# Attention and a two-layer MLP on one core: one PSUM tile with a free list, and key scores in three groups instead of four

## The chip, the cores and the metric

The kernel runs on one core of one Trainium2 chip. The metric is the device time of a run in microseconds (us); the time shown for a kernel is the median of its runs. TensorE is called PE here, VectorE DVE, ScalarE ACT, GpSimd POOL, and SyncE's DMA queue SP.

## The reference

Attention over 8 batches and 12 heads of 448 positions with head size 64, where queries and keys are RMS-normalised, and then two matrix products with a leaky ReLU between them:

```python
q_n, k_n = rmsnorm(q, g_q), rmsnorm(k, g_k)          # 8 x 12 x 448 x 64, over the last axis
scores = 1 / sqrt(64) * q_n @ k_n.T
attn = softmax(scores)
x = (attn @ v), heads joined                          # 3584 x 768
h = x @ w_in                                          # 768 x 2048
out = maximum(0.01 * h, h) @ w_out                    # 2048 x 768, float32
```

## The kernel before

**Units.** The work is cut into 24 units (NU), each of four heads of one batch; three units (NQ) make a batch. For a unit `load` brings 128 x 896 elements of q and of k, DVE and ACT normalise them (`prep_sq`, `prep_ssq`, `prep_rinv`, `prep_norm`, two and more units ahead), a transposing DMA (`prep_trd`) makes `qkT`, and `prep_g` scales the queries. Scores are made transposed, one key tile t of seven (NS) at a time: `score` (L199) issues four 64*64 matmuls for a tile, one for each head, into two banks of PSUM. I call these four a set. `ex` (L218) turns each set into `et` with one exp on ACT, 128 x 896 elements, biased by `eb`, a shift that `shift_max` and `shift_mm` derive from the first set.

**Stages.** A unit has four stages d = 0 to 3. In each, `qk` scores the key tiles `STEPS[d]`, that is 1, 2, 2 and 2 sets, which I call a group; `ex` follows. Then `fill` takes the next `PLAN[u - 3][d]` items (2 or 3 in most stages) from `queue`, the products of the batch before. An item is a block of matmuls on PE: `moe1` (L389) is six 128x448 matmuls into one bank `hps` and a `prelu` on ACT (L383) that empties it; `moe2` (L435) and `seven` (L485) are blocks of eight 128x384 matmuls, emptied by DVE adds and copies and one ACT copy (L518). After each item one small piece of work from the list `jobs` is issued (loads, normalising, `prep_g`, squares). Stage 0 also finishes the unit before: `pv_slot` (attn times v, 28 matmuls, L367, into the two banks of `pslot`), `zcol` (sums of et, into one bank `zc`), `shift_mm`, `pv_out` (L322, ACT copies pslot to SBUF) and `zcol_ln` (L327, ACT reads zc).

**Order.** All instructions are issued in the order of this program (`tc.manual_schedule`), so each engine's queue is written out by hand; semaphores alone decide when each goes.

**PSUM.** There are eight banks of 512 float32 per partition. Before, they are two pools: `slot` hands out pairs of banks under the tag sT with two buffers (four banks), in turn, for score sets, pslot and one sum; `aux` hands out single banks, four buffers in turn, for everything else. From the last batches on `hold` takes the four banks into a list, and `drop` gives them back.

Of the kernel before, what the change touches and what calls it, by code (L numbers as in the profile page):

```python
# [18 lines left out]
def kernel(  # L19
# [34 lines left out]

    held = []

    def aux(shape, dtype, name):
        if held:
            return held[0].pop(0)
        return psum.tile(shape, dtype, tag="aux", bufs=4, name=name)  # L60

    def hold():
        if not held:
            banks = [psum.tile([P, 512], FP32, tag="aux", bufs=4, name=f"bank{i}") for i in range(4)]
            held.append(banks)

    def drop(bank):
        if held:
            held[0].append(bank)

# [96 lines left out]
    def prep_norm(u, c=ALL, tis=BOTH):  # L167
        n = c[1] - c[0]
        for ti in tis:
# [3 lines left out]
                buf(u, "rinv")[:, ti, :, c[0]:c[1], None].broadcast_to([P, 2, n, D]), op=ALU.mult)  # L173

    def prep_tr(u, ti, copies):
        tp = aux([P, NS, P], FP16, "tp")
        for (lo, hi), copy in copies:
            for x in range(lo, hi):
                nc.tensor.transpose(tp[:, x, :], buf(u, "n16")[:, ti, x].rearrange("p a d -> p (a d)"), ident16)
            copy(buf(u, "qkT")[:, ti, lo:hi], tp[:, lo:hi], ti == 0)  # L180

    def prep_trd(u):
# [7 lines left out]
    def kT(u, r, a, t):  # L190
        return buf(u, "qkT")[64 * a:64 * a + 64, 1, t, 64 * r:64 * r + 64]

    def slot():
        return psum.tile([P, 2, 512], FP32, tag="sT", bufs=2, name="sT")

# [12 lines left out]

    def ex(u):
        s = st[u]  # L210
        if "et" not in s:
            s["et"] = epool.tile([P, NS, 2, S], FP16, tag="et", name="et")
        for t, sT in s["sT"]:
            if isinstance(sT, list):
                for a in range(2):
                    nc.scalar.activation(s["et"][:, t, a], sT[a][:, 0:S], AF.Exp, bias=s["eb"], scale=1.0)
            else:
                nc.scalar.activation(s["et"][:, t], sT[:, :, 0:S], AF.Exp, bias=s["eb"], scale=1.0)  # L218

    def score0(u):  # L220
        banks = [aux([P, 512], FP32, "s0") for a in range(2)]
        score(u, 0, banks)
        st[u]["sT"] = [(0, banks)]
# [16 lines left out]
    def shift_bank(u):  # L240
        st[u]["pb"] = aux([P, 512], FP32, "pb")

    def shift_mm(u):
        s = st[u]
        if u > 0 and "pslot" in st[u - 1]:
            pb = st[u - 1]["pslot"][:, :, S:S + 64]
            for x in range(2):
                nc.tensor.matmul(pb[:, x], onesp, s["dg"][:, 64 * x:64 * x + 64], start=True, stop=True)
            nc.vector.tensor_reduce(s["spare"][:, 510:511], pb, axis=AXL.XY, op=ALU.max)  # L249
        else:  # L250
            if "pb" not in s:
                shift_bank(u)
            pb = s["pb"]
            nc.tensor.matmul(pb[:, 0:P], onesp, s["dg"], start=True, stop=True)
            nc.vector.tensor_reduce(s["spare"][:, 510:511], pb[:, 0:P], axis=AXL.X, op=ALU.max)
        s["eb"] = small.tile([P, 1], FP32, tag="eb", name="eb")
        nc.vector.tensor_scalar(s["eb"], s["spare"][:, 510:511], -1.0, DELTA, op0=ALU.mult, op1=ALU.add)
# [41 lines left out]
    def zcol(u):  # L299
        s = st[u]  # L300
        s["zc"] = aux([P, 512], FP32, "zc")
        ets = z_tiles(u)
        for i, e in enumerate(ets):
            for y in range(2):
                for a in range(2):
                    c = 32 * (2 * y + a)
                    nc.tensor.matmul(s["zc"][c:c + 32, 0:HS], onesr, e[:, a, HS * y:HS * y + HS],  # L307
                                     start=(i == 0), stop=(i == len(ets) - 1))
# [7 lines left out]
    def pv_out(u):  # L316
        s = st[u]
        s["x32"] = zpool.tile([P, 2, S], FP32, tag="x32", name="x32")
        if u in (3, 4, 5, 6):
            nc.vector.tensor_copy(s["x32"], s["pslot"][:, :, 0:S])  # L320
        else:
            nc.scalar.copy(s["x32"], s["pslot"][:, :, 0:S])  # L322

    def zcol_ln(u):
# [24 lines left out]
    def zinv(u):  # L349
        s = st[u]  # L350
        s["rz"] = zpool.tile([P, 2, S], FP32, tag="rz", name="rz")
        if "zslot" in s:
            nc.scalar.activation(s["rz"], s["zslot"][:, :, 0:S], AF.Ln)
            nc.scalar.activation(s["rz"], s["rz"], AF.Exp, bias=0.0, scale=-1.0)
        else:
            for r in range(2):
                nc.scalar.activation(s["rz"][:, r], s["zt"][r][:, 0:S], AF.Ln)
                nc.scalar.activation(s["rz"][:, r], s["rz"][:, r], AF.Exp, bias=0.0, scale=-1.0)

    def pv(u, t0=0, t1=NS):  # L360
        s = st[u]
        if t0 == 0 and "pslot" not in s:
            s["pv"] = [aux([P, 512], FP32, "pv") for r in range(2)]
        for t in range(t0, t1):
# [20 lines left out]
    def moe1(b, ft):  # L385
        xt = xts[b]
        hps = aux([P, 512], FP32, "hps")
        for kt in range(KT):
            nc.tensor.matmul(hps[:, 0:S], win16[:, kt // 2, kt % 2, ts(ft, P)], xt[:, kt // 2, kt % 2],  # L389
                             start=(kt == 0), stop=(kt == KT - 1))  # L390
        prelu(b, gt[:, ft, 64 * (b % 2):64 * (b % 2) + S], hps[:, 0:S])
        drop(hps)
# [32 lines left out]
    def moe2(pair, t, half, part, late=False, cut=8):  # L425
# [3 lines left out]
        if part == 0:  # L429
            ost[1] = aux([P, 512], FP32, "op2")  # L430
        op2 = ost[1]
# [48 lines left out]
    def seven(pair, tt, nxt=None, last=False, mixed=False):  # L480
# [6 lines left out]
        def bank(name):  # L487
            g[name] = aux([P, 512], FP32, name)
            return g[name]
# [115 lines left out]
    def late1(b, tail, after):  # L605
# [32 lines left out]
        def get(n, s):  # L638
            g[n, s] = aux([P, 512], FP32, "hp")
            return g[n, s]  # L640

        def start():
            hold()
            if tail:
                for i in range(2):
                    drop(slot()[:, 0])
            for name in ("u", "v"):
# [52 lines left out]
    def push(b):  # L700
# [32 lines left out]
        else:  # L733
# [13 lines left out]
            "3232", "2222", "3323", "3232", "2322", "4356", "5232")  # L747
    STEPS = ((0,), (1, 2), (3, 4), (5, 6))

    def narrow(u):  # L750
# [35 lines left out]
    with tc.manual_schedule():  # L786
# [5 lines left out]
        load(2)  # L792
        gps = aux([P, 512], FP32, "gps")
        wbank = aux([P, 512], FP32, "warm")
        warm(32, wbank)
# [9 lines left out]
        prep_rinv(0, (0,))  # L805
        nc.vector.tensor_copy(gcol, gps[:, 0:1])
        prep_ssq(0, ALL, (1,))
        prep_rinv(0, (1,))
# [5 lines left out]
        def tr(u, ti, chunks, tp=None):  # L814
            if tp is None:
                tp = aux([P, NS, P], FP16, "tp")
            for c, copy in chunks:
                for x in range(*c):
                    nc.tensor.transpose(tp[:, x, :], buf(u, "n16")[:, ti, x].rearrange("p a d -> p (a d)"), ident16)
                copy(buf(u, "qkT")[:, ti, c[0]:c[1]], tp[:, c[0]:c[1]], ti == 0)  # L820
            return tp

        tr(0, 0, ((CA, acopy),))
        tr(0, 0, ((CB, acopy),))
        tpk = tr(0, 1, ((K0, vcopy),))
        warm(6, wbank)
        prep_sq(1, ALL, (0,))
        qk(0, STEPS[0])
        shift_max(0)
        tr(0, 1, ((K1, acopy),), tpk)  # L830
        prep_sq(1, ALL, (1,))
# [8 lines left out]
        warm(10, st[0]["pb"])  # L840
        shift_mm(0)
        prep_ssq(1)

# [19 lines left out]
        load_w_in(1024, 1024)  # L863
        wb = aux([P, 512], FP32, "warm")
        warm(12, wb)
        qk(0, (2,))
        ex(0)
        warm(8, wb)
        qk(0, (3,))
        ex(0)  # L870
        tr(1, 0, ((ALL, vcopy),))
        tpk = tr(1, 1, ((K0, vcopy),))
# [6 lines left out]
        shift_max(1)  # L879
        vcopy(*k1[0])  # L880
        shift_bank(1)
        qk(0, (5,))
# [24 lines left out]
        qk(1, (2,))  # L907
        warm(6, st[1]["pb"])
        ex(1)
        trn(2, 0, vcopy)  # L910
# [36 lines left out]
        trn(3, 0, vcopy)  # L947
        warm(8, st[2]["pb"])
        trn(3, 1, vcopy)
        xmul(1)  # L950
        prep_ssq(4, ALL, (1,))
        qk(2, (4,))
        ex(2)
        st[2]["zt"] = [aux([P, 512], FP32, "zt") for r in range(2)]
        zsum(2, 0, 3)
# [22 lines left out]
        for ft in range(2):  # L978
            prelu(0, gt[:, ft, 0:S], first[:, ft, 0:S])
        del queue[0:2]  # L980

        for u in range(3, NU):
            for d in range(4):
                if d > 0 or u > 3:
                    qk(u, STEPS[d])
                    if d == 0:
# [9 lines left out]
                        else:  # L996
# [3 lines left out]
                            zinv(u - 1)  # L1000
                    ex(u)
                    if d == 0 and narrow(u - 1):
# [67 lines left out]
                if d == 3 and 6 <= u < NU - 3:  # L1070
                    for ti in range(2):
                        job(prep_sq, u + 3, ALL, (ti,))
                fill(u, d, jobs)
        zsum_slot(NU - 1)
# [38 lines left out]
```

## Time and profile before

| what | value |
| --- | --- |
| runs of the kernel | 417.27, 414.97, 413.72 us; median 414.97 |
| span of the profiled execution | 410.6 us, first to last instruction |
| median of the runs less that span | 4.4 us |
| PE busy | 398.2 us (97%), 3840 matmuls |
| DVE busy | 307.2 us (75%) |
| ACT busy | 298.4 us (73%) |
| POOL busy | 69.1 us (17%) |
| granted TensorE clock, mean | 1.000 |
| exp of a score set (L218) | 166 times, mean 1010 ns |
| score matmuls in PSUM pairs (L199) | 664, mean 363 ns, four at a time |

The profiled execution has no time of its own beside its span; what lies around the span is the 4.4 us between it and the median, which belongs to other executions. Busy times overlap. Durations on ACT and DVE overlap the next instruction's by some 0.1 us, so exps that follow each other start 0.90 us apart. The end of a matmul is modelled; its start is recorded, so distances on PE are taken from start to start. Units 7 to 21 lie between 93 and 330 us of the span; one takes 14.7 to 16.9 us.

### The profile page before, as it was taken

Reading aid. Unit: us, or ns where it says so; the run is one execution under the profiler, and the core shown is the slowest. Engines: PE = TensorE matmul, PEld = TensorE weight load, DVE = VectorE, ACT = ScalarE, POOL = GpSimd, SP = SyncE. Lnnn points to the kernel's source line nnn. Section 1 sums busy time; section 2 is a strip of 40 time slices with the busy share of each in tenths; the row PEclk is TensorE's granted clock in tenths of the full one; section 3 lists DMA queues with packets and bytes.
Section 4 is the critical chain, followed back from the end, with each engine's and each line's share of the span. In section 5 each row is a group of like instructions: output and inputs, shape, how many; then the busy total and the mean of one; then the engine's idle time right before and its main releaser. Section 6 shows DMA issues by size and latency. Waiting matters only on the chain.

```text
span 410.6 us, 9395 instructions
## 1 busy us (share of the span) xinstructions
PE 398.2 (97%) x3840; PEld 219.7 (54%) x3840; DVE 307.2 (75%) x490; ACT 298.4 (73%) x470; POOL 69.1 (17%) x70
## 2 busy tenths in 40 slices
PE   8689999999999999999999999999999999999996
PEld 7455444454445544555445544455445557558963
DVE  5997789999788766767669667678568788658772
ACT  5998977677887699777986779967986657653600
POOL 1886433100020200020020200003001202000000
PEclk9999999999999999999999999999999999999999
DMA  5999999999565885577666896667662460032014
GB/s 192 264 255 253 232 234 236 232 190 200 136 156 95 232 224 106 149 196 169 155 151 77 216 201 143 164 127 170 196 114 46 121 152 17 7 80 77 2 44 111
DMA packets 72526, 62.87 MB, mean 153 GB/s; under 512 B 36388, under 2 KB 67620, under 8 KB 72484
## 3 DMA queue, kind: packets, MB, share of 16 engines
q1 hardware_dynamic: 61888, 50.08, 47.6%
q0 software_dynamic: 10272, 11.80, 18.4%
q8 instruction: 30, 0.49, 0.5%
q10 hardware_dynamic: 324, 0.39, 0.3%
q14 instruction: 12, 0.10, 0.1%
HBM read 45.61 MB, written 11.01 MB: 138 GB/s over the span
## 4 chain that ended last, share of the span: by engine, by line
PE 90%; DVE 4%; ACT 3%; DMA 1%; issue 1%; SPq 0%; DVEq 0%
PE hps L389 28%; PE sT L199 10%; PE sT L367 6%; PE op L435 6%; PE mc L485 5%; PE ma L485 5%; PE bank L485 5%; PE md L485 5%; PE bank L617 5%; PE zc L307 3%; PE mb L485 3%; ACT et L218 2%; PE sT L485 2%; PE bank L435 1%; DVE n L171 1%; DMA rk<-in_k_dram 1%
## 5 line engine op out<-in xcount | busy, mean ns | idle before, releaser
L218 ACT ACTIVATE et<-sT,eb 128x896 f16<-128x896 f32 x166 | 159.6, 1010 | 25.8 <-PE sT L199 13.5
L389 PE MATMUL hps<-xt,win 128*128 128x448 f16 x600 | 120.8, 353 | 0.0
L389 PEld LDWEIGHTS <-win 128*128 128x128 f16 x612 | 56.7, 98 | 57.9 <-issue 9.9
L383 ACT ACTIVATE gt<-hps 128x448 f16<-128x448 f32 x100 | 53.9, 558 | 3.8 <-PE hps L389 3.2
L199 PE MATMUL sT<-qkT 64*64 64x448 f16 x664 | 52.3, 363 | 4.0 <-ACT et L218 3.2
L159 DVE TENSOR_REDUCE ssq<-sq 128x14 f32<-128x896 f32 (+2 forms) x49 | 50.2, 1057 | 0.8 <-ACT sq L148 0.8
L485 PEld LDWEIGHTS <-sa 128*128 128x128 f16 x352 | 32.8, 98 | 26.0 <-issue 5.8
L128 POOL DMA_DIRECT2D vt<-in_v_dram x24 | 17.9, 746 | 166.4 <-PE sT L367 166.0
L322 ACT COPY x<-sT 128x896 f32<-128x896 f32 x16 | 14.5, 907 | 29.8 <-DVE sT L249 27.5
L199 PEld LDWEIGHTS <-qkT 64*64 64x64 f16 x672 | 15.4, 104 | 37.2 <-issue 32.5
L485 PEld LDWEIGHTS <-gt 128*128 128x128 f16 x264 | 25.3, 98 | 18.4 <-issue 2.1
L347 POOL TENSOR_TENSOR xt<-x,rz 128x896 f16<-128x896 f32 x9 | 19.5, 2170 | 80.8 <-DMA rz<-zs 73.5
L236 DVE TENSOR_REDUCE sT<-sT 128x1 f32<-128x896 f32 x22 | 24.1, 1096 | 11.4 <-PE sT L199 11.3
L367 PE MATMUL sT<-et,vt 64*64 64x448 f16 x560 | 29.9, 349 | 0.0
L171 DVE TENSOR_TENSOR n<-rq,rinv 128x896 f16<-128x896 f32 (+2 forms) x25 | 26.3, 1055 | 3.2 <-ACT rinv L165 3.2
L435 PE MATMUL op<-wout,gt 128*128 128x384 f16 x160 | 28.4, 327 | 0.0
L171 DVE TENSOR_TENSOR n<-rk,rinv 128x896 f16<-128x896 f32 (+2 forms) x26 | 27.5, 1065 | 0.0
L292 DVE TENSOR_TENSOR ea<-ea,et 128x896 f16<-128x896 f16 x25 | 15.6, 625 | 15.2 <-ACT et L218 14.3
L367 PEld LDWEIGHTS <-vt 64*64 64x64 f16 x672 | 20.3, 107 | 10.6 <-issue 0.4
L435 PEld LDWEIGHTS <-gt 128*128 128x128 f16 x192 | 17.7, 98 | 13.8 <-issue 3.2
L485 PE MATMUL ma<-wout,gt 128*128 128x384 f16 x128 | 23.5, 326 | 0.0
L292 DVE TENSOR_TENSOR ea<-et 128x896 f16<-128x896 f16 x14 | 9.4, 672 | 11.9 <-ACT et L218 11.9
(144 smaller groups left out, 548.4 us busy)
## 6 DMA issues: line engine op xcount, KB each, us to landing
rq<-in_q_dram SPq DMA_DIRECT2D x24, 448.0 KB, 3.9
rk<-in_k_dram SPq DMA_DIRECT2D x24, 448.0 KB, 4.9
out_dram<-ost SPq DMA_DIRECT2D x52, 192.0 KB, 3.5
rz<-zs SPq DMA_DIRECT2D x80, 112.0 KB, 2.3
vt<-in_v_dram POOLq DMA_DIRECT2D x24, 224.0 KB, 5.2
win<-in_moe_w_in_dram POOLq DMA_DIRECT2D x8, 384.0 KB, 14.3
wout<-in_moe_w_out_dram POOLq DMA_DIRECT2D x2, 1536.0 KB, 28.9
out_dram<-ost SPq DMA_DIRECT2D x4, 96.0 KB, 2.1
```

The source lines that it names most:

```text
L159: nc.vector.tensor_reduce(buf(u, "ssq")[:, ti, :, c[0]:c[1]], buf(u, f"sq{ti}")[:, :, c[0]:c[1]], axis=AXL.X, op=ALU.add)
L171: nc.vector.tensor_tensor(buf(u, "n16")[:, ti, c[0]:c[1]].rearrange("p s a d -> p a s d"), src[:, :, c[0]:c[1]], buf(u, "rinv")[:, ti, :, ...
L199: nc.tensor.matmul(banks[a][64 * r:64 * r + 64, 0:S].rearrange("p (t x) -> p t x", t=NS), kT(u, r, a, t), qT(u, r, a), start=True, stop=True)
L218: nc.scalar.activation(s["et"][:, t], sT[:, :, 0:S], AF.Exp, bias=s["eb"], scale=1.0)
L236: nc.vector.tensor_reduce(s["spare"][:, 511:512], sT[:, :, 0:S], axis=AXL.XY, op=ALU.max)
L292: nc.vector.tensor_tensor(s["ea"], s["et"][:, 0] if t == 1 else s["ea"], s["et"][:, t], op=ALU.add)
L367: nc.tensor.matmul(s["pv"][r][64 * a:64 * a + 64, 0:S], vts[u % NV][64 * r:64 * r + 64, a, t], s["et"][64 * r:64 * r + 64, t, a], start=(t ...
L383: nc.scalar.activation(dst, src, AF.Prelu, bias=0.0, scale=1.0, alpha=0.01)
L389: nc.tensor.matmul(hps[:, 0:S], win16[:, kt // 2, kt % 2, ts(ft, P)], xt[:, kt // 2, kt % 2], start=(kt == 0), stop=(kt == KT - 1))
L435: nc.tensor.matmul(op2[:, 0:HC], gt[:, ft, ds(col(t), P)], wout16[:, ft, ds(HC * half, HC)], start=(i == 0), stop=(i == FT - 1))
L485: nc.tensor.matmul(bank[:, 0:HC], a[:, f], b[:, f], start=(first and f == 0), stop=(f == HF - 1), skip_group_check=not first)
L617: nc.tensor.matmul(bank[:, HX * i:HX * i + HX].rearrange("p (t x) -> p t x", t=NS), w, x[:, kt], start=start, stop=(kt == HK - 1), skip_gr ...
```

## The change

All eight banks become one tile `banks`, with views `single` (a bank) and `double` (an aligned pair), and a list `free` of banks in the order in which they were given back. `aux` takes a bank, `slot` takes a pair of free neighbours, `drop` returns either; each place that reads a bank for the last time now drops it. Until unit 7 banks 0 to 3 are for `aux` and 4 to 7 for `slot`, as two separate halves; from unit 7 on (`shared`) both take from all eight. `slot` takes the pair whose later-freed bank was freed longest ago; `aux` prefers a bank whose neighbour is in use.

In units 7 to 21 (`tripled`) the sets are grouped by `TRIPLES`: key tile 0 in stage 0, tiles 1 to 3 in stage 1, none in stage 2, tiles 4 to 6 in stage 3. After a group of three the first two exps are issued at once, as before; the third is joined to the first entry of `jobs`, so that it comes after the first item of the stage. Which items and other jobs a stage has does not change.

```diff
-    held = []
-    def aux(shape, dtype, name):
-        if held:
-            return held[0].pop(0)
-        return psum.tile(shape, dtype, tag="aux", bufs=4, name=name)
...
+    banks = psum.tile([P, 8, 512], FP32, tag="banks", name="banks")
+    single = [banks[:, i] for i in range(8)]
+    double = [banks[:, 2 * i:2 * i + 2] for i in range(4)]
+    free = [3, 0, 2, 1, 4, 5, 6, 7]
+    shared = []
+
+    def mine(i):
+        return shared or i < 4
+
+    def aux():
+        can = [i for i in free if mine(i)]
+        if shared:
+            can = [i for i in can[:-1] if i ^ 1 not in free] or can
+        free.remove(can[0])
+        return single[can[0]]
+
+    def slot():
+        if shared:
+            can = [i for i in free if i ^ 1 in free]
+            last = {i // 2: n for n, i in enumerate(free) if i in can}
+        else:
+            last = {i // 2: n for n, i in enumerate(free) if i >= 4 and i ^ 1 in free}
+        x = min(last, key=lambda i: last[i])
+        for i in (2 * x, 2 * x + 1):
+            free.remove(i)
+        return double[x]
...
-    def ex(u):
+    def ex(u, most=NS):
...
-        for t, sT in s["sT"]:
+        for t, sT in s["sT"][:most]:
...
                 nc.scalar.activation(s["et"][:, t], sT[:, :, 0:S], AF.Exp, bias=s["eb"], scale=1.0)
+                drop(sT)
+        s["sT"] = s["sT"][most:]
...
             nc.scalar.copy(s["x32"], s["pslot"][:, :, 0:S])
+        drop(s["pslot"])
...
         def start():
-            hold()
             if tail:
-                for i in range(2):
-                    drop(slot()[:, 0])
+                shared.append(b)
...
     STEPS = ((0,), (1, 2), (3, 4), (5, 6))
+    TRIPLES = ((0,), (1, 2, 3), (), (4, 5, 6))
+
+    def tripled(u):
+        return 7 <= u < NU - 2
...
         for u in range(3, NU):
             for d in range(4):
+                if u == 7 and d == 0:
+                    shared.append(u)
                 if d > 0 or u > 3:
-                    qk(u, STEPS[d])
+                    qk(u, (TRIPLES if tripled(u) else STEPS)[d])
...
-                    ex(u)
+                    ex(u, 2)
...
+                if st[u]["sT"]:
+                    jobs[0:1] = [also(lambda: ex(u), *jobs[0:1])]
                 fill(u, d, jobs)
```

More of the change, by code (lines that the diff above doesn't have):

```diff
@@ L53, with drop @@
     psum = ctx.enter_context(tc.tile_pool(name="psum", bufs=1, space=bass.MemoryType.PSUM))
-    held = []
-    def aux(shape, dtype, name):
-        if held:
-            return held[0].pop(0)
-        return psum.tile(shape, dtype, tag="aux", bufs=4, name=name)
[L62 to L69, printed above, removed]
+    banks = psum.tile([P, 8, 512], FP32, tag="banks", name="banks")
[21 more added lines that the diff above has]
+        return double[x]
+    def drop(tile_):
+        for i in range(8):
+            if tile_ is single[i]:
+                assert i not in free
+                free.append(i)
+                return
+        x = [i for i in range(4) if tile_ is double[i]][0]
+        assert 2 * x not in free and 2 * x + 1 not in free
+        free.extend((2 * x, 2 * x + 1))
     ident16 = cst.tile([P, P], FP16)
@@ L173, in prep_norm, with as_tp @@
                 buf(u, "rinv")[:, ti, :, c[0]:c[1], None].broadcast_to([P, 2, n, D]), op=ALU.mult)
+    def as_tp(bank):
+        return bank.bitcast(FP16)[:, 0:NS * P].rearrange("p (t x) -> p t x", t=NS)
     def prep_tr(u, ti, copies):
-        tp = aux([P, NS, P], FP16, "tp")
+        bank = aux()
+        tp = as_tp(bank)
         for (lo, hi), copy in copies:
@@ L180, in prep_tr @@
             copy(buf(u, "qkT")[:, ti, lo:hi], tp[:, lo:hi], ti == 0)
+        drop(bank)
     def prep_trd(u):
@@ L191, in kT @@
         return buf(u, "qkT")[64 * a:64 * a + 64, 1, t, 64 * r:64 * r + 64]
-    def slot():
-        return psum.tile([P, 2, 512], FP32, tag="sT", bufs=2, name="sT")
     def score(u, t, banks):
@@ L216, in ex @@
                     nc.scalar.activation(s["et"][:, t, a], sT[a][:, 0:S], AF.Exp, bias=s["eb"], scale=1.0)
+                    drop(sT[a])
             else:
                 nc.scalar.activation(s["et"][:, t], sT[:, :, 0:S], AF.Exp, bias=s["eb"], scale=1.0)
+                drop(sT)
+        s["sT"] = s["sT"][most:]
     def score0(u):
-        banks = [aux([P, 512], FP32, "s0") for a in range(2)]
+        banks = [aux() for a in range(2)]
         score(u, 0, banks)
@@ L240, in shift_bank @@
     def shift_bank(u):
-        st[u]["pb"] = aux([P, 512], FP32, "pb")
+        st[u]["pb"] = aux()
     def shift_mm(u):
@@ L255, in shift_mm @@
             nc.vector.tensor_reduce(s["spare"][:, 510:511], pb[:, 0:P], axis=AXL.X, op=ALU.max)
+            if u >= 3:
+                drop(pb)
         s["eb"] = small.tile([P, 1], FP32, tag="eb", name="eb")
@@ L300, in zcol @@
         s = st[u]
-        s["zc"] = aux([P, 512], FP32, "zc")
+        s["zc"] = aux()
         ets = z_tiles(u)
@@ L353, in zinv @@
             nc.scalar.activation(s["rz"], s["zslot"][:, :, 0:S], AF.Ln)
+            drop(s["zslot"])
             nc.scalar.activation(s["rz"], s["rz"], AF.Exp, bias=0.0, scale=-1.0)
@@ L357, in zinv @@
                 nc.scalar.activation(s["rz"][:, r], s["zt"][r][:, 0:S], AF.Ln)
+                drop(s["zt"][r])
                 nc.scalar.activation(s["rz"][:, r], s["rz"][:, r], AF.Exp, bias=0.0, scale=-1.0)
@@ L362, in pv @@
         if t0 == 0 and "pslot" not in s:
-            s["pv"] = [aux([P, 512], FP32, "pv") for r in range(2)]
+            s["pv"] = [aux() for r in range(2)]
         for t in range(t0, t1):
@@ L386, in moe1 @@
         xt = xts[b]
-        hps = aux([P, 512], FP32, "hps")
+        hps = aux()
         for kt in range(KT):
@@ L429, in moe2 @@
         if part == 0:
-            ost[1] = aux([P, 512], FP32, "op2")
+            ost[1] = aux()
         op2 = ost[1]
@@ L487, in bank @@
         def bank(name):
-            g[name] = aux([P, 512], FP32, name)
+            g[name] = aux()
             return g[name]
@@ L638, in get @@
         def get(n, s):
-            g[n, s] = aux([P, 512], FP32, "hp")
+            g[n, s] = aux()
             return g[n, s]
         def start():
-            hold()
             if tail:
-                for i in range(2):
-                    drop(slot()[:, 0])
+                shared.append(b)
             for name in ("u", "v"):
@@ L792 @@
         load(2)
-        gps = aux([P, 512], FP32, "gps")
-        wbank = aux([P, 512], FP32, "warm")
+        gps = aux()
+        wbank = aux()
         warm(32, wbank)
@@ L806 @@
         nc.vector.tensor_copy(gcol, gps[:, 0:1])
+        drop(gps)
         prep_ssq(0, ALL, (1,))
@@ L815, in tr @@
             if tp is None:
-                tp = aux([P, NS, P], FP16, "tp")
+                tp = aux()
             for c, copy in chunks:
                 for x in range(*c):
-                    nc.tensor.transpose(tp[:, x, :], buf(u, "n16")[:, ti, x].rearrange("p a d -> p (a d)"), ident16)
-                copy(buf(u, "qkT")[:, ti, c[0]:c[1]], tp[:, c[0]:c[1]], ti == 0)
-            return tp
-        tr(0, 0, ((CA, acopy),))
-        tr(0, 0, ((CB, acopy),))
+                    nc.tensor.transpose(as_tp(tp)[:, x, :], buf(u, "n16")[:, ti, x].rearrange("p a d -> p (a d)"), ident16)
+                copy(buf(u, "qkT")[:, ti, c[0]:c[1]], as_tp(tp)[:, c[0]:c[1]], ti == 0)
+            return tp
+        drop(tr(0, 0, ((CA, acopy),)))
+        drop(tr(0, 0, ((CB, acopy),)))
         tpk = tr(0, 1, ((K0, vcopy),))
         warm(6, wbank)
+        drop(wbank)
         prep_sq(1, ALL, (0,))
@@ L829 @@
         shift_max(0)
-        tr(0, 1, ((K1, acopy),), tpk)
+        drop(tr(0, 1, ((K1, acopy),), tpk))
         prep_sq(1, ALL, (1,))
@@ L841 @@
         shift_mm(0)
+        drop(st[0]["pb"])
         prep_ssq(1)
@@ L863 @@
         load_w_in(1024, 1024)
-        wb = aux([P, 512], FP32, "warm")
+        wb = aux()
         warm(12, wb)
@@ L868 @@
         warm(8, wb)
+        drop(wb)
         qk(0, (3,))
         ex(0)
-        tr(1, 0, ((ALL, vcopy),))
+        drop(tr(1, 0, ((ALL, vcopy),)))
         tpk = tr(1, 1, ((K0, vcopy),))
@@ L880 @@
         vcopy(*k1[0])
+        drop(tpk)
         shift_bank(1)
@@ L908 @@
         warm(6, st[1]["pb"])
+        drop(st[1]["pb"])
         ex(1)
@@ L948 @@
         warm(8, st[2]["pb"])
+        drop(st[2]["pb"])
         trn(3, 1, vcopy)
@@ L953 @@
         ex(2)
-        st[2]["zt"] = [aux([P, 512], FP32, "zt") for r in range(2)]
+        st[2]["zt"] = [aux() for r in range(2)]
         zsum(2, 0, 3)
@@ L979 @@
             prelu(0, gt[:, ft, 0:S], first[:, ft, 0:S])
+        drop(first)
         del queue[0:2]
```

## The prediction

> **What bounds the kernel now.** I read the head of the page first, for the share of each engine, then the line of granted clock, then the chain that ended last.
>
> ```profile
> PE 398.2 (97%) x3840; PEld 219.7 (54%) x3840; DVE 307.2 (75%) x490; ACT 298.4 (73%) x470; POOL 69.1 (17%) x70
> ...
> PEclk9999999999999999999999999999999999999999
> ...
> PE 90%; DVE 4%; ACT 3%; DMA 1%; issue 1%; SPq 0%; DVEq 0%
> ```
>
> TensorE (PE) is busy for 97% of the span at a full granted clock, and 90% of the chain is PE; the DVE and ACT shares of it lie in the first 45 us. In the stretch that the change touches (units 7 to 21, 93 to 330 us) the view of waits of PE lists nothing at all. So time can come only from what PE itself spends, and can be lost only by making PE wait. Next the timeline of PE, unit 10:
>
> ```profile
> 143.58 0.23 PE L248 MATMUL sT<-dg,onesp 128*128 128x64 f16 x2
> 143.65 2.44 PE L389 MATMUL hps<-xt,win 128*128 128x448 f16 x12
> 146.01 0.57 PE L199 MATMUL sT<-qkT 64*64 64x448 f16 x8
> 146.51 3.58 PE L389 MATMUL hps<-xt,win 128*128 128x448 f16 x18
> 150.02 0.57 PE L199 MATMUL sT<-qkT 64*64 64x448 f16 x8
> ...
> 155.78 0.38 PE L199 MATMUL sT<-qkT 64*64 64x448 f16 x4
> 155.99 1.49 PE L367 MATMUL sT<-et,vt 64*64 64x448 f16 x28
> ```
>
> Columns: start, duration, engine, line, operation. A score group (L199) stands between blocks of jobs. A key tile is four 64*64 matmuls that run side by side. Inside a block one 128x448 matmul follows another every 0.189 us (12 in 2.27), and so do the four-matmul sets of L367. Around a group it is slower. The records of the single matmuls at 150 us give: last job matmul 149.741, first set 150.023, second set 150.237, next job matmul 150.528. From the last job matmul before to the first after it is 0.787 us, of which three ordinary steps would be 0.567. So 0.22 us is the price of going from 128*128 to 64*64 and back, whatever the group holds. It is the same to 0.001 in nearly all groups of the stretch (0.761 between 128x384 jobs, whose own step is 0.163).
>
> Last, ACT in the same unit, because it frees the banks:
>
> ```profile
> 144.24 0.91 ACT L322 COPY x<-sT 128x896 f32<-128x896 f32 x1 [2.27 <-DVE sT L249]
> 145.04 1.01 ACT L218 ACTIVATE et<-sT,eb 128x896 f16<-128x896 f32 x1
> 145.94 0.36 ACT L327 ACTIVATE zs<-zc 128x224 f32<-128x224 f32 x1
> 146.18 0.56 ACT L383 ACTIVATE gt<-hps 128x448 f16<-128x448 f32 x1
> 146.60 0.41 ACT L332 ACTIVATE zs<-zs 128x224 f32<-128x224 f32 x1
> 146.88 0.56 ACT L383 ACTIVATE gt<-hps 128x448 f16<-128x448 f32 x1
> ```
>
> When the group at 146.01 starts, ACT still owes the release of zc (to 146.30) and of the two job banks (to 146.74 and 147.45). Before the change nobody minds: score slots are banks of their own.
>
> **The change part by part.** (1) *One group fewer in each of units 7 to 21.* Sets, matmuls, exps and their order in a unit stay; nothing is added on any engine, and no DMA moves. A third set should follow the second at the 0.189 of a steady run, as in L367. Group of three: 0.787 + 0.189 = 0.976. A unit had 3 x 0.787 = 2.361; it gets 2 x 0.976, plus one ordinary step of 0.189 where the group was: 2.141. Saved: 0.220. Between 128x384 jobs: 2.283 against 2 x 0.950 + 0.163, again 0.220. Times 15 units: **3.30 us**. No row shows a third score set. The bounds are the two rows nearest: 0.189, and 0.213 (second after first), which costs 0.024 more for each of 30 groups and leaves 2.6. I take 0.189, since by the second set the switch is over.
>
> (2) *The third pair of banks of the first group of a unit.* A group of three takes six of eight banks. Its first pair is that of pslot, free after the copy L322; the second that of the first set, free after its exp; the third comes from the free list, and what it held is read off the changed program's order. The third set is wanted 0.40 after the group's start (0.213 + 0.189). PE follows a release by 0.05: in unit 12 the exp ends at 176.94 and the set starts at 176.99. Up to this point a unit has the order it had, so the release times are those of the trace:
>
> - Units 10 and 16: zc and the first of the two jobs. Its prelu ends at 146.74 (241.13), so PE can go on at 146.79 (241.18), wanted at 146.41 (240.81). Stall 0.38 and 0.37, and 0.024 more for the step after a stalled set (0.306 against 0.282 in unit 12): **0.80** together. Behind the waiting set stand the next job on PE and its prelu on ACT; both move by the same 0.4 and nothing waits for them sooner.
> - Units 12 and 18: zc, whose Ln ends at 177.19. The second set already waits here today (0.912 instead of 0.761), so the third is wanted at 177.18 and can go at 177.24: **0.06** each, 0.12.
> - Units 8, 11, 14, 17, 20: the second prelu of three jobs. Ready at 115.03 against 115.03 in unit 8; 161.78 against 161.88 in 11; 209.43 against 209.43 in 14; 256.18 against 256.28; 303.82 against 303.83. Nothing, with no room.
> - Units 7, 9, 13, 15, 19, 21: 0.1 to 0.8 to spare.
>
> (3) *The third exp after the first job's prelu.* ACT runs three exps (0.90 each) after a group instead of two, at the last group of a unit 0.90 more than before. Today ACT reaches that group late: in unit 10 the group is at 152.90, its exps start at 153.70, because ACT is behind from the group in the middle. That group is gone, so in the changed order only the last job's prelu (hps ends near 152.8, 0.43 of ACT) stands before the exps, and they start at about 153.2: 0.90 more work, 0.5 sooner. At d = 3 the job that the exp is joined to is prep_sq on ACT, behind it in the queue and counted in this; at d = 1 it is prep_g on DVE, which does not wait for it. The 0.4 left over goes into ACT's idle time before the next copy L322: 0.38 in units 11 and 17, 0.72 in 8, 1.2 in 14 and 20, 2 and more in the rest. Cost: 0.0, at most 0.05 in 11 and 17, which have 0.10 to spare. If that cover were gone, the late copy would delay Ln, prelus and so the third pair, as in the slower rival. PE needs the last et tile 1.13 after the start of L367 (six sets of 0.189); by the same walk the third exp of unit 10 ends some 0.8 before that. The jobs' own banks come free from the first two exps, over 1 us before their turn.
>
> (4) *The second group of three* (d = 3) gets banks that were freed at least one whole job (1.13 or 1.31) earlier, by a prelu, a DVE add or an ACT copy; with ACT not behind there, 0. (5) *The free list elsewhere* (units 0 to 6 keep the same four banks; units 22, 23 and the tail get eight instead of six): PE has no wait in the tail now that banks would end, so 0. The 22 waits of PE for its own older matmuls disappear; the groups that carry them show no gap, so 0.
>
> Here the Trainium skill, page "TensorEngine Tiling (Array Packing)", section "Performance Considerations", warns that tiling speeds up TensorE but not the emptying of PSUM, which may become the bottleneck. In unit 10 (141.1 to 155.8) ACT is busy for 12.38 of 14.70 us, so not the bound. By the rule the group would gain nothing and the time would stay at 415.0.
>
> Sum: 3.30 - 0.80 - 0.12 = 2.38 us. The profiled execution spans 410.6; the median of the runs is 414.97, 4.35 above it, which I leave as it is. 410.6 - 2.4 = 408.2, and 408.2 + 4.35 = **412.6 us** (-0.6%). This kernel's measurement tells about 1% (4.15 us) from no change.
>
> **The rivals.** *All of the gain, no wait*: if ACT, relieved of the middle group, reaches d = 0 earlier, units 10 and 16 do not stall. Against: the copy there waits 2.27 for DVE, not for ACT. 414.97 - 3.30 = 411.7.
>
> *Slower: ACT comes to the copy L322 one exp late in every unit.* Place: the third set of each first group; then the release is 0.90 later. Stalls from the times above, in units 7 to 21: 0.24, 0.90, 0.51, 1.28, 0.80, 0.96, 0.14, 0.90, 0.79, 1.27, 0.80, 0.95, 0.14, 0.89, 0.51 = 11.1. Less 3.3: 7.8 slower, 422.8. It eats the gain from a lateness of 0.28 and is over 1% slower from 0.64. For it: five units have no room at all. Against: the idle before L322.
>
> *The switch is not a fixed price*: the third set pays like a fresh one, 0.282 instead of 0.189 in 30 groups (2.8 us), and the gain of 3.3 is 0.5, less the 0.9 of stalls: 415.4. Against: L367, which runs 28 such matmuls after a single score set at 0.189 a set.
>
> *Faster by over 1%*: the waits of PE for itself do cost in the first 45 us, where PE is not steady. 22 at the 0.22 of a full stop would be 4.8; with 2.4 that is 407.8. Against: DVE and ACT set the end there.
>
> **How the numbers follow.** Forecast 0.50, whole gain 0.13, switch not fixed 0.15, slower rival 0.12, faster rival 0.10. Forecast, whole gain and switch lie within 1%: 0.78. Bounds: at the low end the whole gain, 411.7, and the spread of a median of few runs (413.7 to 417.3) takes it to 410.6; at the high end the switch case with 0.05 to 0.1 of lateness in the five units without room, 416.
>
> **What would show it.** Group of three at 0.98 (0.95) us in the records, twice in a unit, and 30 of them; 0.40 more in the first group of units 10 and 16; d = 3 groups unstalled; the idle before L322 in units 11 and 17 near 0. I am wrong if PE's view of waits names ACT at score groups in units 8, 11, 14, 17, 20, if the third set comes later than 0.213 after the second without a wait, or if PE waits within the jobs.

## The result and the profile after

The changed kernel takes 419.18 us (median of 4 runs, 418.34 to 419.36) against 414.35 us (4 runs). The ratio is 1.0107, with a 95% interval of 1.0065 to 1.015: slower by some 4.4 us (2.7 to 6.2 by the interval; the medians differ by 4.8), where 2.4 us faster was forecast. Its profiled execution spans 416.6 us (418.34 with what lies around the span) and holds the clock (0.999 granted in the mean). Line numbers below are those of the changed kernel: L222 score sets (L199 before), L242 exp (L218), L414 prelu (L383), L516 matmuls of `seven` (L485), L497, L500, L503 the DVE sums `s1`, `s2`, `s3` (L466, L469, L472), L376 the product of x32 and rz (L347), L523 DVE adds (L492).

From the page, PE's line and the line of the chain:

```profile
PE 396.9 (95%) x3840; PEld 223.6 (54%) x3840; DVE 310.3 (74%) x490; ACT 299.2 (72%) x470; POOL 68.9 (17%) x70
...
PE 72%; ACT 10%; DVE 10%; DMA 5%; issue 2%; SPq 0%; DVEq 0%; ACTq 0%
```

PE is busy for less time than before (396.9 against 398.2), and yet the kernel is slower: the chain runs through PE for 72% instead of 90%, and ACT and DVE have 10% each. The first line of PE's view of waits (line, awaited, us in total, times, longest) says where. It did not exist before, when the view was empty for units 7 to 21 (a `...` marks lines left out):

```profile
PE banks L516 <- DVE sa L500: 6.1, 3, 2.1
```

Three waits, 2.1 us each, of a job and not of a score group. They are in units 8, 14 and 20, the last units of three batches, where the jobs pass from `moe1` to `seven`. The timeline around the first, PE, ACT, DVE and POOL in turn:

```profile
118.84 1.46 PE L516 MATMUL banks<-wout,gt 128*128 128x384 f16 x8
120.14 0.81 PE L516 MATMUL banks<-tw,sa 128*128 128x384 f16 x4
123.01 0.82 PE L516 MATMUL banks<-tw,sa 128*128 128x384 f16 x4 [2.06 <-DVE sa L500]
...
118.25 0.60 ACT L414 ACTIVATE gt<-banks 128x448 f16<-128x448 f32 x1
118.68 1.07 ACT L242 ACTIVATE et<-banks,eb 128x896 f16<-128x896 f32 x1
119.57 0.62 ACT L414 ACTIVATE gt<-banks 128x448 f16<-128x448 f32 x1
...
120.22 2.28 DVE L497 TENSOR_TENSOR sa<-gt 128x512 f16<-128x512 f16 x1 [1.14 <-ACT gt L414]
122.53 0.42 DVE L500 TENSOR_TENSOR sa<-sa,gt 128x512 f16<-128x512 f16 x1
...
120.15 2.06 POOL L376 TENSOR_TENSOR xt<-x,rz 128x896 f16<-128x896 f32 x1 [7.26 <-DMA rz<-zs]
```

And the same place before the change, DVE and then POOL (its times are 1.2 us earlier there):

```profile
118.20 0.43 DVE L466 TENSOR_TENSOR sa<-gt 128x512 f16<-128x512 f16 x1 [0.33 <-ACT gt L383]
118.66 0.43 DVE L469 TENSOR_TENSOR sa<-sa,gt 128x512 f16<-128x512 f16 x1
119.00 0.55 DVE L507 COPY ost<-ma 128x384 f32<-128x384 f32 x1
119.47 1.85 DVE L472 TENSOR_TENSOR sa<-gt 128x512 f16<-128x512 f16 x1
...
118.95 2.08 POOL L347 TENSOR_TENSOR xt<-x,rz 128x896 f16<-128x896 f32 x1 [7.28 <-DMA rz<-zs]
```

The third exp (118.68) stands between the last two prelus of stage 1. The last prelu therefore ends at 120.19. `s1` needs it, and starts at 120.22 instead of the 119.4 that corresponds to the 118.20 of before. In those 0.8 us the POOL product has begun, and `s1`, which takes 0.43 elsewhere, takes 2.28, until the product is over. `s2` stands behind it on DVE, and PE, in the middle of the next job, waits for `s2`. Before the change it was `s3` that fell under the product (1.85), which nobody needed soon.

In the record of single matmuls the three gaps are 2.385, 2.369 and 2.369 us, less an ordinary step of 0.163 each: 6.63 together. With the rest at the forecast's own steps, -3.30 for the groups and 1.04 for stalls at them (0.45 in each of units 10 and 16, 0.055 in each of 12 and 18, 0.04 in 8, 14 and 20 together), the sum is +4.37. The trace says the same directly: from the first score set of unit 7 to that of unit 22 it takes 241.15 us, before the change 236.78.

The two spans differ by 5.9. The other 1.6 lie outside these units: 1.3 before unit 7 and 0.25 behind unit 21. A small part of that belongs to the free list, 0.27 at 35 us and the 0.25 at the end, as the first experiment shows; the rest differs from profile to profile (unit 7 begins between 93.3 and 94.5 us in the ten with the list, at 92.9 and 93.2 in the two without), and its cause stays open.

### The profile page after: what moved, and what is told of

Same layout as the page of the kernel before. It is cut to its first block, busy times and chain, and to the rows that moved or that the text cites. A ratio compares the mean times of both kernels' runs of the same rounds, so it can differ in the third digit from the quotient of the medians.

```text
span 416.6 us, 9411 instructions
## 1 busy us (share of the span) xinstructions
PE 396.9 (95%) x3840; PEld 223.6 (54%) x3840; DVE 310.3 (74%) x490; ACT 299.2 (72%) x470; POOL 68.9 (17%) x70
## 4 chain that ended last, share of the span: by engine, by line
PE 72%; ACT 10%; DVE 10%; DMA 5%; issue 2%; SPq 0%; DVEq 0%; ACTq 0%
PE banks L516 22%; PE banks L420 22%; PE banks L222 7%; PE banks L648 6%; ACT et L242 6%; PE banks L398 5%; PE banks L466 4%; DMA qkT<-n 3%; PE banks L335 2%; ACT gt L414 2%; DVE n L192 2%; DVE sa L497 2%; DVE ssq L180 1%; DMA rk<-in_k_dram 1%; DMA out_dram<-ost 1%
## 5 line engine op out<-in xcount | busy, mean ns | idle before, releaser
L242 ACT ACTIVATE et<-banks,eb 128x896 f16<-128x896 f32 x166 | 160.3, 1015 | 29.3 <-PE banks L222 16.6
L420 PE MATMUL banks<-xt,win 128*128 128x448 f16 x612 | 122.2, 353 | 0.0
L414 ACT ACTIVATE gt<-banks 128x448 f16<-128x448 f32 x104 | 56.7, 565 | 5.8 <-PE banks L420 4.6
L222 PE MATMUL banks<-qkT 64*64 64x448 f16 x672 | 50.8, 362 | 4.3 <-ACT et L242 3.4
L516 PE MATMUL banks<-tw,sa 128*128 128x384 f16 x264 | 47.4, 326 | 6.1 <-DVE sa L500 6.1
L516 PEld LDWEIGHTS <-sa 128*128 128x128 f16 x352 | 33.1, 98 | 31.5 <-DVE sa L500 7.3
L523 DVE TENSOR_TENSOR ost<-banks,ost 128x384 f32<-128x384 f32 x55 | 30.4, 553 | 17.2 <-PE banks L516 16.0
L398 PE MATMUL banks<-et,vt 64*64 64x448 f16 x672 | 37.0, 349 | 0.1
L222 PEld LDWEIGHTS <-qkT 64*64 64x64 f16 x672 | 17.9, 104 | 35.4 <-issue 28.4
L516 PEld LDWEIGHTS <-gt 128*128 128x128 f16 x264 | 25.5, 98 | 18.0 <-issue 1.4
L262 DVE TENSOR_REDUCE banks<-banks 128x1 f32<-128x896 f32 x22 | 24.1, 1096 | 14.7 <-PE banks L222 10.9
L466 PE MATMUL banks<-wout,gt 128*128 128x384 f16 x192 | 34.1, 327 | 0.0
L376 POOL TENSOR_TENSOR xt<-x,rz 128x896 f16<-128x896 f32 x9 | 19.4, 2159 | 81.8 <-DMA rz<-zs 74.3
L516 PE MATMUL banks<-wout,gt 128*128 128x384 f16 x176 | 32.4, 326 | 0.0
L192 DVE TENSOR_TENSOR n<-rq,rinv 128x896 f16<-128x896 f32 (+2 forms) x25 | 27.3, 1095 | 2.9 <-ACT rinv L186 2.9
L350 ACT COPY x<-banks 128x896 f32<-128x896 f32 x16 | 14.5, 906 | 20.6 <-DVE banks L275 20.6
L192 DVE TENSOR_TENSOR n<-rk,rinv 128x896 f16<-128x896 f32 (+2 forms) x26 | 27.5, 1065 | 0.0
```

The costliest lines, as they stand in the source:

```text
L192: nc.vector.tensor_tensor(buf(u, "n16")[:, ti, c[0]:c[1]].rearrange("p s a d -> p a s d"), src[:, :, c[0]:c[1]], buf(u, "rinv")[:, ti, :, ...
L222: nc.tensor.matmul(banks[a][64 * r:64 * r + 64, 0:S].rearrange("p (t x) -> p t x", t=NS), kT(u, r, a, t), qT(u, r, a), start=True, stop=True)
L262: nc.vector.tensor_reduce(s["spare"][:, 511:512], sT[:, :, 0:S], axis=AXL.XY, op=ALU.max)
L398: nc.tensor.matmul(s["pv"][r][64 * a:64 * a + 64, 0:S], vts[u % NV][64 * r:64 * r + 64, a, t], s["et"][64 * r:64 * r + 64, t, a], start=(t ...
L414: nc.scalar.activation(dst, src, AF.Prelu, bias=0.0, scale=1.0, alpha=0.01)
L466: nc.tensor.matmul(op2[:, 0:HC], gt[:, ft, ds(col(t), P)], wout16[:, ft, ds(HC * half, HC)], start=(i == 0), stop=(i == FT - 1))
```

## The experiments

Each verdict is a ratio to runs of the kernel before on the same chip, whose median was 414.2 to 414.3. The theory, as formed from the two traces: **the third exp delays the last prelu of stage 1; the DVE sum that needs it falls under the POOL product; PE waits for the next sum.** The rivals were that the free list costs (A), that groups of three cost everywhere (B), that the group itself and not the exp's place delays PE (C), that the delay alone makes the wait without POOL (D), that any POOL work at that moment costs the same (E), and that the exp's sharing the first job's place is to blame (F).

**The list alone.** Every unit keeps four groups.

```diff
-        return 7 <= u < NU - 2
+        return False
```

> The changed kernel with its free list, but four groups in every unit (1, 2, 2, 2 sets) as before the change. Theory (the third exp goes ahead of the last prelu of stage 1 in units 8, 14 and 20, the DVE sum L497 that needs this prelu then falls under the POOL product, and PE waits 2.2 us for L500, three times; the rest of the change does what was forecast): the time of the kernel before, 414.4 within 1 us, groups of two at 0.787 and 0.761, and no gap over 0.3 us between L516 matmuls. Rival A (the free list itself costs, by its order of banks, as the 0.3 to 0.6 us in the first 40 us and the 0.7 us in unit 6 may hint): 1 to 2 us above the kernel before.

Measured: 414.14, ratio 1.0017 (0.9989 to 1.0045). In PE's view of waits no L516 is left, and units 7 to 21 take 236.90 us against 236.78: what was lost there is not the list's. (One gap is over the 0.3 expected: 0.43 in unit 9, behind a normalisation that took 1.88 under a POOL product instead of 1.08.) But the list is not quite free. All ten kernels of this text that have it show one more wait, of PE at 35 us, for a DVE instruction that empties a bank:

```profile
PE banks L204 <- DVE qkT L801: 0.3, 1, 0.3
```

The step there is 0.55 instead of 0.28, and from unit 22 to the end the ten take 0.24 to 0.27 more; the two kernels with two pools (the one before, and the one with an exp done twice, below) show neither. That is some 0.5 us. As 1 to 2 us of the kernel's time rival A is not excluded by the interval alone, which reaches 1.9; as the cause of the 4.4 it falls.

**Three units left out.**

```diff
-        return 7 <= u < NU - 2
+        return 7 <= u < NU - 2 and u not in (8, 14, 20)
```

> The changed kernel, but units 8, 14 and 20 keep four groups. Theory: the three gaps of 2.2 us are gone. 12 groups fewer save 12 x 0.22 = 2.64, units 10, 12, 16, 18 give back 0.92 (units 10 and 16 at 1.422 for the group, 12 and 18 at 1.156): 1.7 below the kernel before, 412.7. Rival A (list): 1 to 2 us above that. Rival B (groups of three cost everywhere): above the kernel before by some 12/15 of what the change lost, 418.

Measured: 412.07, ratio 0.9967 (0.9929 to 1.0005). The gaps are gone; the first groups of units 10 and 16 are 1.424, those of 12 and 18 1.16. The whole loss sat in three units: units 7 to 21 now take 1.75 us less than before. What the other twelve gain, some 1.4 by the ratio, agrees with the 1.7 of the steps, though its interval touches 1. Rival B falls.

**The third exp one item later** (in stage 1 of units 8, 14 and 20).

```diff
-                    jobs[0:1] = [also(lambda: ex(u), *jobs[0:1])]
+                    n = 1 if d == 1 and u in (8, 14, 20) else 0
+                    jobs[n:n + 1] = [also(lambda: ex(u), *jobs[n:n + 1])]
```

> The changed kernel, but in stage 1 of units 8, 14 and 20 the third exp comes after the second item (after its prelu) instead of after the first. Theory: the prelu that L497 needs is 0.9 earlier, so L497 (0.43) starts at about 119.6 of unit 8, before the POOL product at 120.15; if L500, some 0.45 behind, also starts before it, the three gaps are gone and the time is 412.0 (3.30 less 0.92 below the kernel before); L500 may just miss, then it is the one that takes 2 us and the gaps stay near 2. Rival C (the place of the exp is nothing, the group of three delays PE there): gaps unchanged, 418 to 419.

Measured: 413.04, ratio 0.9997 (0.9968 to 1.0026): the slowdown is gone, but not all of the gain is there. Its DVE and POOL in unit 8:

```profile
119.07 0.43 DVE L497 TENSOR_TENSOR sa<-gt 128x512 f16<-128x512 f16 x1 [0.53 <-ACT gt L414]
119.53 0.43 DVE L500 TENSOR_TENSOR sa<-sa,gt 128x512 f16<-128x512 f16 x1
119.87 0.55 DVE L538 COPY ost<-banks 128x384 f32<-128x384 f32 x1
120.34 1.83 DVE L503 TENSOR_TENSOR sa<-gt 128x512 f16<-128x512 f16 x1
...
119.58 2.31 POOL L376 TENSOR_TENSOR xt<-x,rz 128x896 f16<-128x896 f32 x1 [7.24 <-DMA rz<-zs]
```

`s1` and `s2` are done before POOL matters, as before the change, and `s3` takes the blow again. PE still loses 1.05 us in units 14 and 20, by another way that I had not expected: the add L523 stands behind `s3` and is late by it, and now PE wants its bank (2.0 us in two waits in the view of waits). In the two pools four banks went round among the jobs; in the shared list the group of three has taken six of the eight banks, and the next job gets one of the two left, which were freed last. Rival C (gaps unchanged) falls.

**The product on DVE.** In units 8, 14 and 20 the product goes to DVE in stage 3; the third exp stays.

```diff
-                if d == 1 and narrow(u - 1) and not 5 <= u < 8 and ADDED.get(u, 0) < 4:
+                if d == 1 and narrow(u - 1) and not 5 <= u < 8 and ADDED.get(u, 0) < 4 and u not in (8, 14, 20):
                     xmul_pool(u - 1)
...
+                if d == 3 and u in (8, 14, 20):
+                    job(xmul_sb, u - 1)
```

> The changed kernel, but in units 8, 14 and 20 the product L376 of the unit before runs on DVE in stage 3 instead of on POOL from stage 1; the third exp stays where the change put it. Theory: L497 still starts late (about 120.2 in unit 8) but takes 0.43 instead of 2.28, so PE waits only some 0.3 us each time: 1.4 below the kernel before, 413.0. Rival D (the lateness of the prelu alone makes the wait, POOL has no part): gaps stay at 2.2, 418 to 419.

Measured: 412.55, ratio 0.9967 (0.9933 to 1.0000; 413.0 was expected). `s1` is as late as in the changed kernel and takes 0.43:

```profile
119.00 0.43 DVE L497 TENSOR_TENSOR sa<-gt 128x512 f16<-128x512 f16 x1 [1.14 <-ACT gt L414]
119.46 0.42 DVE L500 TENSOR_TENSOR sa<-sa,gt 128x512 f16<-128x512 f16 x1
...
119.94 0.82 PE L516 MATMUL banks<-tw,sa 128*128 128x384 f16 x4 [0.21 <-DVE sa L500]
```

The gap is 0.54 instead of 2.38. The delay of the prelu alone is worth 0.38 in each unit; the other 1.84 come from POOL. Rival D falls.

**Half of the product on POOL.** The other half of the columns goes to DVE in stage 3.

> The changed kernel, but in units 8, 14 and 20 POOL multiplies only half of the columns of L376 and DVE does the other half in stage 3. Theory (the DVE sum lasts until the POOL product is over): POOL takes 1.0 to 1.1 instead of 2.06, the sum 1.2 to 1.4 instead of 2.28, and the gap falls from 2.22 to between 1.0 and 1.3 in each of the three units: 414.9 to 415.8. Rival D: gaps stay at 2.2, 419. Rival E (any POOL work at that moment costs the same): 2.2, 419.

Measured: 412.95, ratio 0.9973 (0.9951 to 0.9995). The gap is 0.80, less 0.163: 0.64, below the 1.0 to 1.3 expected (and the time below the 414.9 to 415.8), because the shorter product also began earlier in relation to `s1` (0.72 instead of 0.07 before it):

```profile
120.02 0.69 DVE L497 TENSOR_TENSOR sa<-gt 128x512 f16<-128x512 f16 x1 [1.14 <-ACT gt L414]
...
119.30 1.12 POOL L376 TENSOR_TENSOR xt<-x,rz 128x448 f16<-128x448 f32 x1 [6.62 <-DMA rz<-zs]
```

The product ends at 120.42 and `s1` at 120.71, 0.29 later; in the changed kernel at 122.21 and 122.50, again 0.29. The sum does its work after the product, whatever the product's length. Rival E falls: half of the work on POOL cost PE less than a third.

**The kernel before, one exp done twice.** Nothing of the change is in this kernel; a second exp to the same output stands where the change has its third.

```diff
+                if d == 1 and u in (8, 14, 20):
+                    jobs[0:1] = [also(lambda: again(u), *jobs[0:1])]
                 fill(u, d, jobs)
```

> The kernel before, with two pools and four groups; in stage 1 of units 8, 14 and 20 the second exp of the group is done a second time, to the same output, after the first item, where the change has its third exp. Theory (0.9 us of ACT ahead of the last prelu pushes the DVE sum of that prelu under the POOL product): in unit 8 the sum starts at about 119.0, POOL at 118.95, so it ends near 121.0 and its successor near 121.4, while PE wants that at 119.97: a gap of some 1.5 in three units, 4.4 slower, 418.7. Rival D (lateness alone, POOL has no part): successor done at 119.9, no gap, 414.3. Rival A (banks and free list): no gap, 414.3.

Measured: 420.01, ratio 1.0172 (1.0117 to 1.0226). In unit 8 it is the same picture, with the two pools and four groups (lines are this kernel's; L471 and L474 are `s1` and `s2`):

```profile
118.70 2.20 POOL L352 TENSOR_TENSOR xt<-x,rz 128x896 f16<-128x896 f32 x1 [7.25 <-DMA rz<-zs]
...
118.89 2.30 DVE L471 TENSOR_TENSOR sa<-gt 128x512 f16<-128x512 f16 x1
121.22 0.42 DVE L474 TENSOR_TENSOR sa<-sa,gt 128x512 f16<-128x512 f16 x1
...
121.71 0.82 PE L490 MATMUL mb<-tw,sa 128*128 128x384 f16 x4 [1.79 <-DVE sa L474]
```

So 0.9 us of ACT ahead of that prelu is enough, without groups of three and without the list. It cost 5.8 us by the medians and 7.1 by the ratio, more than the 4.4 expected; in the profile units 7 to 21 take 8.2 more. The gap in unit 8 was 1.95 instead of 1.5, but those in 14 and 20 only 1.07, for PE came later there: the doubled exp holds the score slot of the next group (0.88 us in each), which I had not seen. Nor had I seen that other products of POOL move and catch other DVE work: in units 9 and 18 a normalisation (L171) takes 2.59 and 2.97 instead of 1.08, and PE loses 1.0 and 1.4 behind it. These terms make up the 8.2.

**Three exps at once**, before the first item:

```diff
-                    ex(u, 2)
+                    ex(u)
```

> The changed kernel, but all three exps of a group are issued at once, before the first item. Theory: ACT has the same work ahead of the last prelu of stage 1, so the gaps of 2.2 in units 8, 14 and 20 stay: 419. Rival F (the exp shares the first job's place, and that place is what costs): gaps gone, 412.

Measured: 419.39, ratio 1.013 (1.0093 to 1.0168), gaps of 2.38 in the same three units. The "first job's place" is not to blame; any place before the last prelu is. Rival F falls.

**Three edits together**: the later exp, the product on DVE, and the bank beside zc kept free in stage 0 of units 10 and 16, so that the third pair waits for the Ln of zc instead of a prelu.

```diff
+        can = [i for i in free if mine(i) and i not in kept]
...
         drop(s["zc"])
+        if u + 1 in (10, 16):
+            n = free[-1] ^ 1
+            assert n in free
+            free.remove(n)
+            free.append(n)
+            kept.extend((n, n ^ 1))
...
+                if d == 1:
+                    kept.clear()
```

> The changed kernel with three edits: in stage 1 of units 8, 14 and 20 the third exp after the second item; their product L376 on DVE in stage 3; and in units 10 and 16 the bank next to zc is kept free in stage 0, so that the third pair waits for the Ln of zc and not for a prelu. Theory: no gap between L516 matmuls, first groups of units 10 and 16 at 0.98 to 1.05 instead of 1.42, units 12 and 18 still 1.16; 3.30 less 0.12 to 0.2 below the kernel before: 411.1. Rival A (list): 1 to 2 us above that. Rival B: no better than the third-exp and the product edits alone, 412.5 to 413.

Measured: 410.37, ratio 0.9919 (0.9892 to 0.9945): faster than both kernels, by 3.4 us against the one before. No L516 gap is left. The first groups of units 10 and 16 are 1.11 instead of 1.42: the third set no longer waits, but 0.14 has moved to the job after it, which wants the bank of the late prelu. Unit 18 is at 1.33, more than expected; it is 1.16 in the same kernel without the later exp, and why is not shown.

**Two controls.** The list and the product on DVE with four groups:

> The free list with four groups in every unit (as in the run of the list alone), and in units 8, 14 and 20 the product L376 on DVE in stage 3 instead of on POOL. It asks whether the gain of the version with three edits comes from the grouping or from the product's new place. Theory (before the change PE never waited for the sums under the product, since L497 was done before it): nothing to gain, 414.2 within 1 us. Rival G (the product's place is itself worth 1 to 2 us, and the groups of three little): 412 to 413.

Measured: 413.89, ratio 0.9993 (0.9974 to 1.0012). The new place of the product is worth nothing by itself; the gain is that of the groups. Rival G falls. And the three edits without the later exp:

> The version with three edits, but with the third exp back at the place that the change gave it (after the first item). Theory (with POOL out of the way the late prelu costs PE only the 0.38 that the run with the product on DVE showed, in each of three units): 1.1 above the version with three edits, 411.5, and three gaps of 0.54 between L516 matmuls. Rival H (the place of the exp no longer matters): 410.4.

Measured: 411.73, ratio 0.9947 (0.9927 to 0.9967), with three gaps of 0.54. As expected, the late prelu still costs 0.38 in each of three units when POOL is out of the way; rival H falls. The gaps show it; the two medians, 1.4 apart, were not measured side by side and would not show it alone.

## Why the prediction was wrong, point by point

- **What bounds the kernel**: right. PE bounds it, and time is lost only where PE waits.
- **(1) The price of a group**: right to the third digit. Groups of three that do not stall take 0.976 to 0.977 and 0.950. That the 0.22 for each group fewer is real time shows in the version with three edits (0.9919) against its control with four groups (0.9993); with the bad units merely left out the interval of the ratio (0.9929 to 1.0005) still reaches 1. The rival in which the switch is not a fixed price falls.
- **(2) The third pair**: right. Units 10 and 16 stall for 0.446 each (0.40 forecast), 12 and 18 for 0.055 (0.06), 8, 14 and 20 for 0.013 (0, "with no room"), the others for nothing:

```profile
149.01 1.21 PE L222 MATMUL banks<-qkT 64*64 64x448 f16 x12
```

  This is the changed kernel's group at unit 10 in the timeline; an unstalled one has 0.76 to 0.78 in this column.
- **(3) The third exp: the step that failed.** I wrote "Cost: 0.0". I followed the 0.9 us on ACT to the next copy L350 (L322) and to the banks of the jobs, that is to what ACT frees, and never asked who reads what the prelu writes. Behind it stood DVE's `s1`, behind `s1` on its engine `s2`, and for that PE was waiting. The slack before the change could be read: `s1` waited 0.33 for the prelu (the bracket at 118.20), so it already ran the moment the prelu ended, and `s2` was done at 119.09, where PE wanted it at 119.97. Of these 0.88 the missing group of stage 2 takes 0.4 (PE comes 0.60 sooner, less 0.19 for the longer group before). A delay of 0.8 then costs some 0.3; the run with the product on DVE showed 0.38. The other 1.84 in each unit is a fourth engine: POOL's product began 0.75 after `s1`, and it holds any such sum that comes later until it is over. The row that showed it stood in the trace of before: L472, in its 128x512 form five times 0.42 and, the three times that it ran under a product, 1.3 to 1.85.
- **(4) and the cover that I named**: the prediction asked for slack where banks are freed. It should have asked, for each instruction pushed back, what else becomes late. "If PE waits within the jobs" was given as a sign of being wrong, without a price.
- **(5) The free list elsewhere**: put at 0, and some 0.5: the wait of 0.27 at 35 us, in the units that were to keep "the same four banks", and 0.25 in the tail. Inside the units it showed in the run with the later exp, where a job waited 1.05 for a bank freed last. The faster rival, which hoped for a gain here, falls with the list alone.
- **The slower rival** had the right sign and the wrong place: the copy L350 one exp late. The idle time before it did take the exp, as forecast (PE's waits at score groups hold 1.04 us in all). The lateness went to the other reader of ACT.

## What to carry to other kernels

A group of instructions that makes PE change its tile shape has a price of its own (0.22 us here), which is read from start to start across the group, and fewer groups saved exactly that. When something is added to the queue of an engine that is not the bound, list every instruction behind it, and for each one all of its readers, not only what it frees. An instruction that starts shortly ahead of a long operation on a neighbouring engine (here 0.75 us) and is pushed back by more than that must be counted with what is left of that operation, if the runs show that the one holds the other.

## What the runs showed of the hardware

DVE work waits for a POOL product to end, but not all DVE work. Under a product L497, L503 (L472 before) and the normalisation L192 (L171), which read two operands from SBUF, took up to 2.31, 1.85 and 2.97 us instead of 0.42, 0.42 and 1.08. The add L523 and the copy L538, which read PSUM, kept their 0.55 and 0.56 in all cases (six and three such, before the change). A sum of squares (L159 before) that reads a single operand from SBUF was not held either: its first of two here took 1.07, its usual time, and ran almost wholly under a product.

```profile
47.71 1.69 POOL L152 TENSOR_TENSOR sq<-rq 128x896 f32<-128x896 f32 x1
48.38 2.07 DVE L159 TENSOR_REDUCE ssq<-sq 128x14 f32<-128x896 f32 x2
```

It is no sharing of speed: the sum ended 0.29 after the product, for a product of 2.06 and for one of 1.12. The other held work of the profiles agrees: whenever it had started, the sum ended 0.28 or 0.29 after the product and the normalisation 0.94 or 0.95, each some 0.14 less than its own 0.42 or 1.08. So held work does all of itself, but for that 0.14, once the product is over. The trace of before shows the reverse as well: a product that started 0.22 after a normalisation took 2.83 instead of 2.08.

```profile
277.29 1.09 DVE L171 TENSOR_TENSOR n<-rq,rinv 128x896 f16<-128x896 f32 x1 [0.31 <-ACT rinv L165]
277.51 2.83 POOL L347 TENSOR_TENSOR xt<-x,rz 128x896 f16<-128x896 f32 x1 [8.62 <-DMA rz<-zs]
```

The Trainium skill, page "GPSIMD Engine Reference", section "Specifications", states that GpSimd's SBUF interfaces are shared with VectorE and contend with DVE instructions in a two-port mode or with two SBUF inputs; this case's runs agree, and add the price.

After a release PE starts 0.05 us later, in the changed kernels too (three edits, unit 10: a prelu ends at 146.21, the block that waits for its bank starts at 146.26).
